# Half-F rows of w4 taken for four token tiles in one excursion, with a fixed order of w3, w4 and attention tiles

## The chip, the cores and the metric

The kernel runs on one core of a Trainium2 chip. The metric is the device time of one execution in microseconds (us), the median of several. Executions of one kernel scatter by about 1 us (0.4%). The differences at stake are 0.1 to 0.9 us, most of them below what timing alone resolves, so the text uses a second measure, read from the trace of one profiled execution of each kernel. It is called the **stretch**: from the start of the first projection matmul with the weights `wkg` (the matmuls of `wq` for the first tiles come before it) to the start of the last matmul of all. It leaves out the head and the 2.8 us tail. Times within a trace are counted from the start of its own execution; where two traces are compared to a fraction of a us, their heads (before 12.83, after 12.58) have to be taken off, and the text says where it does so.

Engines are named as the profile names them: PE (TensorE matmuls), PEld (TensorE weight loads), DVE (VectorE), ACT (ScalarE), POOL (GpSimd), SP (SyncE). The kernel takes PSUM, which receives the results of matmuls, as eight **banks** of 512 float32 columns in each of 128 partitions.

## The reference, cut to what matters

```python
# S = 2048 tokens, D = 640, F = 1728; 32 heads of 20
q, k, v = split(x @ wqkv);  pq, pk = phi(q), phi(k)
kv = sum_s pk v^T;  z = sum_s pk
a  = (pq @ kv / (pq . z)) @ wo                       # linear attention
x1 = x + shift(gelu(layernorm(x) @ w1)) @ w2
b  = x1 + gelu(layernorm(x1) @ w3) @ w4              # F = 13 * 128 + 64
out = g * a + (1 - g) * b
```

F is thirteen times 128 and a half: the last 64 rows of `w4` (and columns of `w3`) are the **half-F** part. There are 16 token tiles of 128, in four chunks of four tiles.

## The kernel before

Everything is written as *items* in streams. At build, a list scheduler takes the streams' items one at a time, guided by a small model of the engines' times, and so fixes the order of the instructions on every engine. At run time nothing is reordered: an item that the model put too early makes its engine wait. This is the model's wait rule and the rule of choice (`cp` is the longest path of item durations behind an item):

```python
for w in waits:          # in the model: when may this instruction start?
    tw = self.ev_time.get(w, 0.0) + (170.0 if w[0] == sem else SEM_LAT)   # same engine 170 ns, else 60
...
if sem.startswith("d:") and nbytes < 0:                # a DMA transpose
    self.eng_free[eng] = t + 1350.0
    end = t + 2800.0
...
key = (max(est, t_pe), 0 if it["dur"] == 0.0 else 1, -cp[n])              # smallest key is emitted next
```

One token tile of w4 is a `w4_tile`: thirteen matmuls of 512 columns and thirteen of 128. The half-F part comes first, in a `w4_half` for two tiles at a time, with 64-row matmuls in pairs (rows 0 to 63 serve one tile, rows 64 to 127 the other):

```python
def w4_half(t):                                   # t = 0, 2, 4, ... 14: eight excursions
    pr = (t % 4) // 2
    for i in range(2):
        b = pair(); bs += [b, b + 1]; w4_banks[t + i] = (b, b + 1)
    bank_hold.update(bs)                          # four banks held
    for i, (n0, n1) in enumerate(((0, 512), (512, D))):
        for par in range(2):
            rows = slice(64 * par, 64 * par + 64)
            jobs.append((ps[:, bs[2 * par + i], 0:n1 - n0], h2h[rows, t // 4, 128 * pr:128 * (pr + 1)], w4[rows, KFF, n0:n1]))
    ... # one matmul per job, start=True, stop=False

def w4_tile(t):                                   # 13 + 13 matmuls of 128 rows, start=False
    ...
    stt(x_tok[:, t, :], psf[:, 512 * b1:512 * b1 + D], stg[:, 3, t:t + 1], abx[:, sa, :], ALU.mult, ALU.add)  # one eviction; tile 15 in two
```

The attention tile and what must be there before it:

```python
qt_tile(t):  DMA transpose  pqnT[:, :, tile t] <- pq_tok[:, t, :]      # queue of SP; after W2 tile 15 and transpose 15 of xn
a_tile(t):   10 matmuls of pqnT[:, j, tile t] with M_sb; eviction into abx on VectorE
```

`pqnT` needs `pq_tok` divided by its denominators (query normalisation: `qs`, then `qn`, on VectorE). And the SP queue serves the transposes in order: the first `pqnT` comes behind the last of 16 transposes of the normalised `x1` (`xnT<-xn`), which hangs on this chain: W2 tile (PE) → its eviction into `x_tok` (VectorE) → squares (ScalarE) → statistics (GpSimd) → normalisation into `xn`, a **ring of 3 buffers** (GpSimd) → transpose (SP's queue).

## Time and profile before

| | before |
|---|---|
| median of 3 runs | 265.46 us (265.42 to 265.71) |
| profiled execution, span | 264.6 us |
| PE busy | 258.2 us, 98% of the span |
| share of PE in the chain that ended last | 96% |
| stretch | 248.967 us |
| PE waits within the stretch | none |

The first three lines are the page's span, its busy table and its table of the chain that ended last.

```profile
span 264.6 us, 4264 instructions
PE 258.2 (98%) x1675; PEld 136.4 (52%) x1707; DVE 145.9 (55%) x242; ACT 107.6 (41%) x216; POOL 91.1 (34%) x148
PE 96%; DMA 1%; issue 1%; ACT 0%; DVE 0%
```

The groups of instructions by line with shapes kept apart: line, engine, operation, out<-in, partitions x elements, count | busy us, mean ns of one | idle us before them and its releaser.

```profile
L1085 PE MATMUL ps<-w_84,h2h 64*128 64x512 bf16 x16 | 3.1, 386 | 0.0
...
L645 DVE SCALAR_TENSOR_TENSOR x_tok<-ps,stg,abx 128x640 bf16<-128x640 f32 x15 | 13.2, 883 | 48.8 <-PE ps L1103 48.8
```

The mean of the matmuls (386 ns) is no cost: matmuls overlap, and their ends are modelled. What a matmul costs is the distance between starts, 216 ns for 512 columns and 56 ns for 128 in this trace. That agrees with the Trainium skill, "TensorE: Matmul & The Clock Gate" (Wait — 56ns, not 53.3ns?), which gives 215.7 and 55.6 ns for back-to-back matmuls on the warm array.

The cost at issue stands in the timeline of PE around an excursion (start us, duration us, engine, line, operation, count):

```profile
173.34 1.24 PE L606 MATMUL ps<-xnT,w_58 128*128 128x512 bf16 x5
174.51 0.45 PE L1085 MATMUL ps<-w_84,h2h 64*128 64x512 bf16 x4
174.89 1.47 PE L1103 MATMUL ps<-w_84,h2T 128*128 128x512 bf16 x6
```

Five matmuls of 216 ns from 173.34 should let the next start at 174.42; the 64-row pair starts at 174.51, about 0.09 us late. A pair of 512 columns and a pair of 128 take 0.216 + 0.056 us (the two matmuls of a pair, on different rows, start 3 ns apart here), so the next full matmul should start at 174.78; it starts at 174.89. Read from single starts in nanoseconds, an entry costs 95 to 97 ns, an exit 92 to 93, and the second pair after an entry and the second matmul after an exit start another 10 to 11 late (227 ns after the one before them instead of 216). These are **mode switches**; the Trainium skill, "TensorEngine Tiling (Array Packing)" (Key Properties), says that changing the tiling mode drains TensorE, and gives no number. Eight such excursions exist.

The waits of PE: engine, line, waited for: us in total, times, longest us.

```profile
PE ps L834 <- POOL ones_c L665: 1.6, 1, 1.6
PE ps L1103 <- issue: 0.3, 2, 0.2
...
PE ps L606 <- issue: 0.2, 1, 0.2
```

The first belongs to the head, as does the line left out. The two with "issue" are lone gaps of exactly one matmul (216 ns) where a matmul's record is missing from the trace (1675 records of 1707), not waits. So after its head PE never waits in this kernel. The first attention tile:

```profile
138.72 1.03 PE L606 MATMUL ps<-xnT,w_58 128*128 128x512 bf16 x4
139.58 2.60 PE L606 MATMUL ps<-M_sb,pqnT 128*128 128x512 bf16 x14
```

It starts directly after the w3 matmuls before it. Its transpose is the first in this line of the timeline of SP (merged, eight of them):

```profile
135.28 10.54 SPq L279 DMA_TRANSPOSE pqnT<-pq_tok  x8
```

It was issued at 135.28 us and took 2.7 us to land, so it was there at about 138.0: a slack of 1.5 us, which no table of waits shows.

### The profile page before, as it was taken

The page shows a single profiled execution, that of the slowest core. Times are in us where ns is not written, and L with a number is a line of the kernel's source. Part 1 is how long each engine was busy: PE and PEld are TensorE (multiplying, and loading weights), DVE is VectorE, ACT ScalarE, POOL GpSimd, SP SyncE. Part 2 cuts the span into 40 slices and gives each one's busy share as a digit, 9 for nine tenths or more (in the row PEclk, how much of TensorE's full clock was granted, in tenths as well). Part 3 has the DMA queues.
Part 4 walks back from the last instruction along what each step waited for, and adds up shares of the span by engine and source line. Part 5 has one row for each costly group of instructions (what it writes and reads, how often), then busy time and mean ns, then how long its engine had stood idle before and what let it go on. Part 6 is the DMA issues. An engine that isn't in the chain of part 4 may idle for free.

```text
span 264.6 us, 4264 instructions
## 1 busy us (share of the span) xinstructions
PE 258.2 (98%) x1675; PEld 136.4 (52%) x1707; DVE 145.9 (55%) x242; ACT 107.6 (41%) x216; POOL 91.1 (34%) x148
## 2 busy tenths in 40 slices
PE   7999999999999999999999999999999999999996
PEld 3655555555555454554444545554545455545553
DVE  0397877899903797999786886312212121122242
ACT  3486767742365758675661031212211222121000
POOL 4003996849774017487821104001110011021020
DMA  6775898551666895253666731120000200002011
GB/s 203 244 103 147 205 146 149 162 115 24 102 121 104 299 373 82 54 99 60 69 124 124 110 68 25 33 93 0 2 0 0 102 0 0 2 0 99 2 50 50
DMA packets 50595, 24.77 MB, mean 94 GB/s; under 512 B 41996, under 2 KB 49165, under 8 KB 50576
## 3 DMA queue, kind: packets, MB, share of 16 engines
q1 hardware_dynamic: 49328, 21.23, 36.3%
q0 software_dynamic: 1152, 3.28, 5.4%
q8 instruction: 13, 0.21, 0.3%
q14 instruction: 6, 0.05, 0.1%
q10 hardware_dynamic: 96, 0.00, 0.0%
HBM read 12.05 MB, written 2.62 MB: 55 GB/s over the span
## 4 chain that ended last, share of the span: by engine, by line
PE 96%; DMA 1%; issue 1%; ACT 0%; DVE 0%
PE ps L606 60%; PE ps L1103 21%; PE ps L786 8%; PE ps L858 2%; DMA x_tok<-in_A_x_dram 1%; PE ps L1085 1%; PE ps L1025 1%; PE ps L617 1%; PE ps L859 1%; PE ps L944 1%; DVE x_tok L645 0%; PE ps L834 0%; ACT h2T L662 0%; ACT M_sb L662 0%
## 5 line engine op out<-in xcount | busy, mean ns | idle before, releaser
L662 ACT ACTIVATE h2T<-ps 128x512 bf16<-128x512 f32 x52 | 31.0, 597 | 86.5 <-PE ps L606 86.5
L606 PE MATMUL ps<-xnT,w_58 128*128 128x512 bf16 x250 | 59.0, 379 | 0.5
L1103 PE MATMUL ps<-w_84,h2T 128*128 128x128 bf16 (+1 forms) x412 | 58.2, 298 | 0.4 <-issue 0.3
L628 POOL TENSOR_SCALAR abx<-x_tok,stg 128x640 f32<-128x640 bf16 x16 | 13.9, 874 | 107.6 <-DVE x_tok L645 71.0
L1103 PEld LDWEIGHTS ps<-w_84,h2T 128*128 128x128 bf16 x416 | 32.4, 98 | 27.8 <-issue 2.1
L645 DVE SCALAR_TENSOR_TENSOR x_tok<-ps,stg,abx 128x640 bf16<-128x640 f32 (+2 forms) x17 | 14.3, 844 | 50.7 <-PE ps L1103 50.7
L606 PEld LDWEIGHTS ps<-xnT,w_58 128*128 128x128 bf16 x260 | 24.3, 98 | 24.9 <-issue 0.4
L645 DVE SCALAR_TENSOR_TENSOR abx<-ps,stg,abx 128x640 f32<-128x640 f32 x16 | 14.1, 882 | 28.5 <-PE ps L606 25.5
L662 ACT ACTIVATE Er<-ps 128x640 bf16<-128x640 f32 x32 | 22.4, 704 | 12.7 <-PE ps L606 8.5
L662 ACT ACTIVATE hsT<-ps 128x512 bf16<-128x512 f32 (+1 forms) x32 | 18.9, 593 | 14.6 <-PE ps L606 14.3
L661 ACT ACTIVATE junk<-x_tok 128x640 bf16<-128x640 bf16 x32 | 23.6, 736 | 2.0 <-DVE x_tok L643 1.7
L606 PE MATMUL ps<-M_sb,pqnT 128*128 128x128 bf16 (+1 forms) x157 | 23.7, 298 | 0.2
L606 PE MATMUL ps<-w_60,hsT 128*128 128x128 bf16 (+1 forms) x158 | 23.6, 298 | 0.1
L786 PE MATMUL ps<-pk_tok,x_tok 128*128 128x128 bf16 (+1 forms) x156 | 23.3, 297 | 0.2
L606 PE MATMUL ps<-xnT,w_59 128*128 128x512 bf16 x96 | 23.2, 379 | 0.3 <-issue 0.2
L606 PE MATMUL ps<-wkg,xT 128*128 128x131 bf16 (+1 forms) x148 | 22.4, 298 | 0.1
L606 PEld LDWEIGHTS ps<-M_sb,pqnT 128*128 128x128 bf16 x160 | 13.3, 98 | 12.4 <-issue 0.4
L606 PEld LDWEIGHTS ps<-w_60,hsT 128*128 128x128 bf16 x160 | 13.3, 98 | 12.2
L628 POOL TENSOR_SCALAR xn<-x_tok,st_54 128x640 bf16<-128x640 bf16 x16 | 17.4, 1090 | 4.7 <-DMA xnT<-xn 4.6
L606 PE MATMUL ps<-wq,xT 128*128 128x128 bf16 (+1 forms) x118 | 18.2, 298 | 0.1
L628 POOL TENSOR_SCALAR xn<-x_tok,st_55 128x640 bf16<-128x640 bf16 x16 | 16.3, 1028 | 3.6 <-DMA xnT<-xn 3.2
L628 DVE TENSOR_SCALAR Er<-Er 128x640 bf16<-128x640 bf16 x32 | 12.0, 375 | 9.4 <-ACT Er L662 9.2
(74 smaller groups left out, 264.2 us busy)
## 6 DMA issues: line engine op xcount, KB each, us to landing
w_58<-in_B_w_dram SPq DMA_DIRECT2D x1, 2160.0 KB, 8.2
w_84<-in_B_w_dram SPq DMA_DIRECT2D x1, 2080.0 KB, 13.6
x_tok<-in_A_x_dram SPq DMA_DIRECT2D x3, 640.0 KB, 5.5
out_dram<-x_tok SPq DMA_DIRECT2D x3, 640.0 KB, 3.3
wq<-in_A_wqkv_dram SPq DMA_DIRECT2D x5, 160.0 KB, 4.4
wkg<-in_A_wqkv_dram SPq DMA_DIRECT2D x5, 160.0 KB, 4.4
wv<-in_A_wqkv_dram POOLq DMA_DIRECT2D x1, 800.0 KB, 6.3
wo_aug<-in_A_wo_dram POOLq DMA_DIRECT2D x5, 150.0 KB, 5.1
```

Source lines behind the costliest of these rows:

```text
L606: ins = e.matmul(out_ap, l, r, start=(i == 0), stop=(i == n - 1))
L617: ins = e.transpose(o, s_, ident[:])
L628: return engf(lambda e: e.tensor_scalar(out_ap, in_ap, s1, s2, op0, op1), rd, [out_ap], cost=cost)
L645: return dve(lambda e: e.scalar_tensor_tensor(out_ap, in0, scalar, in1, op0, op1), rd, [out_ap], cost=cost)
L661: return act(lambda e: e.activation(out_ap, in_ap, func, bias=bias, scale=scale, accum_out=accum), rd, wr, cost=cost)
L662: return act(lambda e: e.activation(out_ap, in_ap, func, bias=bias, scale=scale), rd, wr, cost=cost)
L786: ins = e.matmul(o, l, r, start=(t0 + q_ == 0), stop=(t0 + q_ == NT - 1))
L858: e.matmul(ps[:, b, 0:512], l, w[:, k, 0:512], start=(k == 0), stop=(k == KD - 1))
L859: return e.matmul(ps[:, b + 1, 0:n2], l, w[:, k, 512:512 + n2], start=(k == 0), stop=(k == KD - 1))
L944: ins = e.matmul(o, l, r_, start=st_, stop=sp_, skip_group_check=True)
L1025: ins = e.matmul(o, l, r, start=st, stop=sp)
L1103: ins = e.matmul(o, l, r, start=False, stop=(i == KFF - 1))
```

## The change

The intent is to halve the mode switches of w4: one excursion for four tiles, so four of eight go. Six banks are then held: one per tile for the 512 columns, and two banks shared by the 128-column tails of tiles t and t+2. With six banks taken, w3 cannot be woven between w4 tiles, so the order is fixed by new dependencies: all of w3 of the next chunk, then the excursion, then the four w4 tiles with one attention tile between. Besides, every w4 eviction is split in two, and one number of the scheduler's model changes: a VectorE instruction that waits on VectorE is modelled with 40 ns of latency where it had 170.

```diff
-                tw = ... + (170.0 if w[0] == sem else SEM_LAT)
+                tw = ... + ((40.0 if eng == "dve" else 170.0) if w[0] == sem else SEM_LAT)
 def w4_half(t):
-        pr = (t % 4) // 2
-        ...                       # two pairs of banks, four jobs
+        b0, b2, bt = pair(), pair(), pair()
+        tiles = [((b0, b2)[i // 2] + i % 2, bt + i % 2, 128 * (i // 2)) for i in range(4)]
+        bank_hold.update((b0, b0 + 1, b2, b2 + 1, bt, bt + 1))
+            for pr in range(2):
+                for par, tail in ((0, False), (1, False), (0, True), (1, True)):
+                    ...           # tail: start=(pr == 0), shares bank bt + par
+                    ...           # else: start=True
 def w4_tile(t):
-        stt(x_tok[:, t, :], psf[...], ...)                              # tile 15 alone in two
+        stt(x_tok[:, t, 0:512], ps[:, b1, 0:512], ...)
+        stt(x_tok[:, t, 512:D], ps[:, b2, q0:q0 + 128], ...)
 # dependencies
-                if c >= 2: deps.append((("w4", 4 * (c - 2) + 3), 0.0))  # w3 chunk c
+                if c >= 2: deps.append((("a", 4 * c - 1), 0.0))
+            if c == 1 and j == KFF - 3: deps.append((("a", 3), 0.0))
-        if t % 2 == 0: IT.add("W4", ("w4h", t), 0.49, ...)
+        if t % 4 == 0:
+            deps4.append((("w3", min(c + 1, NCH - 1), KFF - 1), 0.0))
+            if t == 0: deps4.append((("a", 3), 0.0))
+        elif t + 3 < NT: deps4.append((("a", t + 3), 0.0))
+        if t % 4 == 0: IT.add("W4", ("w4h", t), 0.76, ...)
... (cut)
```

More of the change, by code (lines that the diff above doesn't have):

```diff
@@ L238, in simulate @@
             for w in waits:
-                tw = self.ev_time.get(w, 0.0) + (170.0 if w[0] == sem else SEM_LAT)
+                tw = self.ev_time.get(w, 0.0) + ((40.0 if eng == "dve" else 170.0) if w[0] == sem else SEM_LAT)
                 if tw > t:
@@ L1068, in w4_half @@
         tag_chk("h2T", sl, t // 4)
-        pr = (t % 4) // 2
-        bs = []
-        for i in range(2):
-            b = pair()
-            bs += [b, b + 1]
-            w4_banks[t + i] = (b, b + 1)
-        bank_hold.update(bs)
-        jobs = []
-        for i, (n0, n1) in enumerate(((0, 512), (512, D))):
-            for par in range(2):
-                rows = slice(64 * par, 64 * par + 64)
-                jobs.append((ps[:, bs[2 * par + i], 0:n1 - n0], h2h[rows, t // 4, 128 * pr:128 * (pr + 1)], w4[rows, KFF, n0:n1]))
+        b0, b2, bt = pair(), pair(), pair()
+        tiles = [((b0, b2)[i // 2] + i % 2, bt + i % 2, 128 * (i // 2)) for i in range(4)]
+        for i in range(4):
+            w4_banks[t + i] = tiles[i]
+        bank_hold.update((b0, b0 + 1, b2, b2 + 1, bt, bt + 1))
         def fn(e):
             ins = None
-            for o, l, r in jobs:
-                ins = e.matmul(o, l, r, start=True, stop=False)
+            for pr in range(2):
+                for par, tail in ((0, False), (1, False), (0, True), (1, True)):
+                    rows = slice(64 * par, 64 * par + 64)
+                    bm, bs, q0 = tiles[2 * pr + par]
+                    l = h2h[rows, t // 4, 128 * pr:128 * (pr + 1)]
+                    if tail:
+                        ins = e.matmul(ps[:, bs, q0:q0 + 128], l, w4[rows, KFF, 512:D], start=(pr == 0), stop=False,
+                                       skip_group_check=True)
+                    else:
+                        ins = e.matmul(ps[:, bm, :], l, w4[rows, KFF, 0:512], start=True, stop=False)
             return ins
-        pe(fn, [h2h[:, t // 4, 128 * pr:128 * (pr + 1)], w4[:, KFF, :]], [j[0] for j in jobs], cost=490.0)
+        pe(fn, [h2h[:, t // 4, :], w4[:, KFF, :]], [ps[:, b, :] for b in (b0, b0 + 1, b2, b2 + 1, bt, bt + 1)], cost=760.0)
     def w4_tile(t):
@@ L1094, in w4_tile @@
         a = t % 4
-        b1, b2 = w4_banks.pop(t)
+        b1, b2, q0 = w4_banks.pop(t)
         def grp(o, n0, n1):
@@ L1102, in fn @@
                 for i, (l, r) in enumerate(prs):
-                    ins = e.matmul(o, l, r, start=False, stop=(i == KFF - 1))
+                    ins = e.matmul(o, l, r, start=False, stop=(i == KFF - 1), skip_group_check=(n0 > 0))
                 return ins
@@ L1106, in w4_tile @@
         grp(ps[:, b1, 0:512], 0, 512)
-        grp(ps[:, b2, 0:128], 512, D)
+        grp(ps[:, b2, q0:q0 + 128], 512, D)
         bank_hold.discard(b1)
-        bank_hold.discard(b2)
-        if t == NT - 1:
-            stt(x_tok[:, t, 0:512], ps[:, b1, 0:512], stg[:, 3, t:t + 1], abx[:, sa, 0:512], ALU.mult, ALU.add)
-            stt(x_tok[:, t, 512:D], ps[:, b2, 0:128], stg[:, 3, t:t + 1], abx[:, sa, 512:D], ALU.mult, ALU.add)
-        else:
-            stt(x_tok[:, t, :], psf[:, 512 * b1:512 * b1 + D], stg[:, 3, t:t + 1], abx[:, sa, :], ALU.mult, ALU.add)
+        if a >= 2:
+            bank_hold.discard(b2)
+        stt(x_tok[:, t, 0:512], ps[:, b1, 0:512], stg[:, 3, t:t + 1], abx[:, sa, 0:512], ALU.mult, ALU.add)
+        stt(x_tok[:, t, 512:D], ps[:, b2, q0:q0 + 128], stg[:, 3, t:t + 1], abx[:, sa, 512:D], ALU.mult, ALU.add)
     def out_tiles(t0, t1):
@@ L1171, in _build @@
                 if c >= 2:
-                    deps.append((("w4", 4 * (c - 2) + 3), 0.0))
+                    deps.append((("a", 4 * c - 1), 0.0))
+            if c == 1 and j == KFF - 3:
+                deps.append((("a", 3), 0.0))
             IT.add("W3", ("w3", c, j), 1.08, lambda c=c, j=j: w3_group(c, j), deps)
@@ L1193, in _build @@
         deps4 = [(("a", t), 0.0), (("w3h", c - c % 2), GEL), (("w3", c, KFF - 1), GEL)]
-        if t % 2 == 0:
-            IT.add("W4", ("w4h", t), 0.49, lambda t=t: w4_half(t), deps=deps4)
+        if t % 4 == 0:
+            deps4.append((("w3", min(c + 1, NCH - 1), KFF - 1), 0.0))
+            if t == 0:
+                deps4.append((("a", 3), 0.0))
+        elif t + 3 < NT:
+            deps4.append((("a", t + 3), 0.0))
+        if t % 4 == 0:
+            IT.add("W4", ("w4h", t), 0.76, lambda t=t: w4_half(t), deps=deps4)
         IT.add("W4", ("w4", t), 3.5, lambda t=t: w4_tile(t), deps=deps4)
```

## The prediction

> **What bounds it now.** TensorE. The page's busy table gives PE 258.2 of 264.6 us (98%); the chain that ended last is 96% PE. Busy PE alone proves little, so I read start times of single matmuls: from 7.7 us to the last (261.8 us) they follow at 216 ns (512 columns) or 56 ns (128 columns). Lone 216 ns extras every 7 to 9 us are missing records. The real extras are mode switches, into and out of matmuls on part of the rows or columns. Otherwise only the head (about 6 us) and the tail (2.8 us after the last matmul starts) are lost.
>
> **What it removes.** The half-F matmuls of w4 (64 rows) run as eight excursions of four (groups by line: 32). Before each, the first pair starts 95 to 97 ns late; after it the next 128-row matmul is 92 ns late, the one after another 10. That is about 200 ns each, 1.6 us in all, and agrees with the Trainium skill ("TensorEngine Tiling (Array Packing)", Key Properties: changing tiling mode drains the TensorE). Four excursions of eight do the same work: 4 x 0.2 = 0.8 us goes, all on the critical path. Inside a merged excursion the second 512 pair follows a 128 pair; its weight load (94 ns) may not hide under 55 ns: up to 40 ns each back. Net -0.65 to -0.8 us.
>
> Tails of tiles t and t+2 share a bank, only the first flagged start; this is what the skill's "PSUM — Partial Sum Buffer" (The four PSUM rules) asks. I expect correct results.
>
> **What it adds.** 15 VectorE evictions split in two: 0.76 + 0.35 us instead of 0.88 (last tile against the others). VectorE is about 20% busy after 174 us (stretch table): free.
>
> **What it moves.** With six banks held, w3 of the next chunk no longer interleaves with w4; one attention tile (1.36 us of PE) stands between w4 tiles (3.5 us). Its pair is evicted about 1.1 us after PE: no wait. Before the first three excursions stand w3 groups of 1.08 us with 0.60 us gelu: banks come free in time. Before the last excursion a w4 tile may come directly, one of its six banks still in eviction (0.76 us, starting 0.5 us before PE is done): estimate 0.2 to 0.4 us of PE wait. The half-F of w3 for chunks 2 and 3 probably lands just before a w4 excursion: one direct mode change instead of two, -0.1 us. In the query normalisation phase (118 to 166 us, VectorE 70 to 85% busy) four attention tiles must come before w3 of chunk 1 ends; evictions queue behind VectorE pieces of up to 1.6 us: 0 to 1 us of new waits. The changed VectorE latency in the scheduler's model is nearer the trace (dependent VectorE instructions follow within 40 ns) and reorders earlier phases a little; PE is saturated there either way.
>
> **Sum.** -0.75 - 0.1 + 0.3 = about -0.6 us from 265.5: 264.9 us; range 264.3 to 266.3. Faster by over 2% (under 260.2) needs idle PE time that does not exist: 1%. Slower by over 2% needs a bank or VectorE jam: 3%. Within 2%: 96%.
>
> **What would show it.** 64-row w4 matmuls still 32, in four runs of eight; eight switches of 92 to 97 ns instead of sixteen; PE share 97 to 98%; PE waits on VectorE under 0.5 us, only before the last excursion; 32 x_tok evictions instead of 17.
>
> **What would make it wrong.** PE waiting before an excursion for six banks, or for attention evictions at 140 to 160 us; w3 waiting for normalised input; a reordering in the first 120 us that opens gaps.

## The result, and the profile after

The result is correct. The median of six runs is 265.78 us (265.2 to 266.18), against 265.65 us (265.42 to 266.42) for the kernel before in the same rounds. Ratios here and below are the mean time of one kernel's fast runs over that of the other's of the same rounds, so not quite the ratio of the medians quoted: 0.9999, 95% interval 0.9979 to 1.0018, the same. (Where the text says faster or slower it means that the interval lies on one side of 1.)

```profile
span 264.4 us, 4289 instructions
PE 259.3 (98%) x1707; PEld 136.3 (52%) x1707; DVE 148.6 (56%) x257; ACT 107.7 (41%) x216; POOL 93.8 (35%) x148
PE 91%; POOL 3%; DMA 2%; DVE 1%; issue 0%; SPq 0%; ACT 0%; POOLq 0%
```

PE's share is 98% as before, and its busy time is even 1.1 us longer, because all 1707 records are there this time. Busy time does not show what follows. The Trainium skill, "Perfetto Trace Analysis" (Identifying the Most-Contended Engine), says of another use of it, judging how close a kernel is to roofline, that matmul busy time is not a good measure; here it does not tell a kernel with 0.87 us of waits from one without. The chain that ended last does show something new: 91% PE, and GpSimd, a DMA and SP's queue within it.

The excursions are as intended: 32 half-F matmuls, four runs of eight, eight switches.

```profile
L1086 PE MATMUL ps<-w,h2h 64*128 64x512 bf16 x16 | 2.6, 381 | 0.1
...
L645 DVE SCALAR_TENSOR_TENSOR x_tok<-ps,stg,abx 128x512 bf16<-128x512 f32 x16 | 12.0, 750 | 64.8 <-PE ps L1104 64.8
L645 DVE SCALAR_TENSOR_TENSOR x_tok<-ps,stg,abx 128x128 bf16<-128x128 f32 x16 | 5.6, 350 | 0.0
```

The timeline of PE at the first of them:

```profile
155.71 0.81 PE L606 MATMUL ps<-xnT,w 128*128 128x512 bf16 x3
156.45 0.39 PE L1086 MATMUL ps<-w,h2h 64*128 64x512 bf16 x2
156.68 0.22 PE L1083 MATMUL ps<-w,h2h 64*128 64x128 bf16 x2
156.73 0.38 PE L1086 MATMUL ps<-w,h2h 64*128 64x512 bf16 x2
156.95 0.22 PE L1083 MATMUL ps<-w,h2h 64*128 64x128 bf16 x2
157.10 1.47 PE L1104 MATMUL ps<-w,h2T 128*128 128x512 bf16 x6
```

The second 512 pair starts at 156.73, 56 ns after the 128 pair at 156.68 (first matmul to first matmul), which is the usual distance for 128 columns: its weight load (94 ns in the trace) costs nothing.

But PE now waits in two places. The waits of PE, and the timeline of PE at both places (in brackets: idle before, and the releaser):

```profile
PE ps L834 <- POOL ones_c L665: 1.6, 1, 1.6
PE ps L606 <- DMA pqnT<-pq_tok: 0.5, 1, 0.5
```

```profile
140.51 2.33 PE L606 MATMUL ps<-xnT,w 128*128 128x512 bf16 x10
143.36 1.31 PE L606 MATMUL ps<-M_sb,pqnT 128*128 128x512 bf16 x6 [0.52 <-DMA pqnT<-pq_tok]
...
245.49 0.39 PE L1086 MATMUL ps<-w,h2h 64*128 64x512 bf16 x2
```

The bracket counts from a modelled end; by the distance of starts the first attention tile is **0.681 us** late. The last excursion at 245.49 starts 282 ns late, 95 of them the switch: **0.187 us** of wait. There the timeline of VectorE shows the two evictions of the w4 tile before it from 244.68 to 245.76, as one of the six banks is still to be emptied:

```profile
244.68 1.08 DVE L645 SCALAR_TENSOR_TENSOR x_tok<-ps,stg,abx 128x512 bf16<-128x512 f32 x2 [1.92 <-PE ps L1104]
```

(The view has merged two instructions and prints the shape of the first. Taken singly they are the tile's 512-column eviction, 750 ns from 244.68 to 245.43, and its 128-column eviction, 351 ns from 245.40. The excursion starts 57 ns after the end of the first one.)

Stretch: 248.994 us, 0.027 more than before. So the stretch as a whole gained nothing; whether the merging itself did is what e_split will show. Where the first wait comes from can be followed in the chain of waits in order of time:

```profile
129.21 0.83 ACT junk L661 x2
...
134.19 4.67 POOL xn L628 x4
138.86 0.79 POOL abx L628
...
140.59 2.72 DMA pqnT<-pq_tok
...
143.36 13.16 PE ps L606 x75
```

PE waits for the first `pqnT` transpose, issued at 140.59 (before: 135.28; with the heads taken off, 5.6 us later). It stands in SP's queue behind the last transposes of `xn`, these behind the last four normalisations on GpSimd, these behind statistics of squares that ScalarE made at 129.2. One step earlier still is the eviction of the last W2 tile on VectorE. PE finishes that tile at 125.44; VectorE does this instead of its eviction:

```profile
125.49 1.08 DVE L1045 TENSOR_TENSOR pq_tok<-pq_tok,dnr 128x640 bf16<-128x640 bf16 x1
126.49 0.81 DVE L636 TENSOR_TENSOR qprod<-pq_tok,zb 128x640 f32<-128x640 bf16 x1
127.34 0.82 DVE L1035 TENSOR_REDUCE dnr<-qprod 128x32 f32<-128x640 f32 x1
128.07 0.81 DVE L643 SCALAR_TENSOR_TENSOR x_tok<-ps,x_tok 128x640 bf16<-128x640 f32 x1
```

The last line is the eviction, 2.6 us after PE was done: a query normalisation and the sums of the next stand in front of it.

### The profile page after: what moved, and what is told of

Its sections match the earlier page's. It is cut to its first block, busy times and chain, and to the rows that moved or that the text cites. A ratio compares the mean times of both kernels' runs of the same rounds, so it can differ in the third digit from the quotient of the medians.

```text
span 264.4 us, 4289 instructions
## 1 busy us (share of the span) xinstructions
PE 259.3 (98%) x1707; PEld 136.3 (52%) x1707; DVE 148.6 (56%) x257; ACT 107.7 (41%) x216; POOL 93.8 (35%) x148
## 4 chain that ended last, share of the span: by engine, by line
PE 91%; POOL 3%; DMA 2%; DVE 1%; issue 0%; SPq 0%; ACT 0%; POOLq 0%
PE ps L606 56%; PE ps L1104 21%; PE ps L786 8%; PE ps L858 2%; POOL xn L628 2%; DMA x_tok<-in_A_x_dram 1%; POOL st L636 1%; DMA pqnT<-pq_tok 1%; PE ps L1086 1%; DVE x_tok L645 1%; PE ps L617 1%; PE ps L944 1%; PE ps L859 1%; PE ps L1025 0%; SPq L279 0%
## 5 line engine op out<-in xcount | busy, mean ns | idle before, releaser
L606 PE MATMUL ps<-xnT,w 128*128 128x512 bf16 x360 | 82.6, 379 | 0.0
L1104 PE MATMUL ps<-w,h2T 128*128 128x512 bf16 (+1 forms) x416 | 58.8, 299 | 0.0
L606 PEld LDWEIGHTS ps<-xnT,w 128*128 128x128 bf16 x360 | 33.8, 98 | 36.0 <-issue 0.4
L1104 PEld LDWEIGHTS ps<-w,h2T 128*128 128x128 bf16 x416 | 32.4, 98 | 25.6 <-issue 1.1
L628 POOL TENSOR_SCALAR xn<-x_tok,st 128x640 bf16<-128x640 bf16 x32 | 35.6, 1122 | 6.7 <-DMA xnT<-xn 6.3
L606 PE MATMUL ps<-M_sb,pqnT 128*128 128x512 bf16 (+1 forms) x160 | 24.4, 299 | 0.5 <-DMA pqnT<-pq_tok 0.5
L606 PE MATMUL ps<-w,hsT 128*128 128x512 bf16 (+1 forms) x160 | 24.3, 299 | 0.0
L786 PE MATMUL ps<-pk_tok,x_tok 128*128 128x512 bf16 (+1 forms) x160 | 23.9, 299 | 0.0
L606 PE MATMUL ps<-wkg,xT 128*128 128x512 bf16 (+1 forms) x150 | 22.6, 299 | 0.0
L606 PE MATMUL ps<-wq,xT 128*128 128x512 bf16 (+1 forms) x120 | 18.3, 299 | 0.0
```

The lines of the kernel that those rows point to most:

```text
L606: ins = e.matmul(out_ap, l, r, start=(i == 0), stop=(i == n - 1))
L628: return engf(lambda e: e.tensor_scalar(out_ap, in_ap, s1, s2, op0, op1), rd, [out_ap], cost=cost)
L786: ins = e.matmul(o, l, r, start=(t0 + q_ == 0), stop=(t0 + q_ == NT - 1))
L1104: ins = e.matmul(o, l, r, start=False, stop=(i == KFF - 1), skip_group_check=(n0 > 0))
```

## The experiments

The theory after this reading was: *merging gives about 0.85 us; the 40 ns of the model, not the fixed order, creates the 0.68 us wait; placing the last excursion directly after a w4 tile costs the 0.19.* Rivals: the merged excursion is worth less than it seems (contention, reloads); the wait comes from the new dependencies or the split evictions; PE would have waited anyway. Twelve kernels were run; all gave correct results. One table for all; each is then told by itself. Every ratio is against the kernel before in the same rounds.

| run | what | stretch us | PE waits in the stretch, ns | median us | ratio, 95% |
|---|---|---|---|---|---|
| (before) | | 248.967 | none | 265.65 | 1 |
| (after) | | 248.994 | 681 + 187 | 265.78 | 0.9999 (0.9979 to 1.0018) |
| e_lat | before, 40 ns | 251.368 | 2391 | 269.82 | 1.0139 (1.0118 to 1.0161) |
| e_170 | after, 170 ns | 248.308 | 187 | 265.08 | 0.9962 (0.9944 to 0.9979) |
| e_split | after, excursions cut in two | 249.839 | about 686 + 190 | 266.27 | 1.0014 (0.9998 to 1.003) |
| e_both | after, two dependencies more | 248.370 | 250 (a new one) | 264.99 | 0.9961 (0.9939 to 0.9982) |
| e_lat_hold | e_lat, first attention tile later | 248.969 | none | 265.58 | 0.9988 (0.997 to 1.0006) |
| e_lat_ring | e_lat, ring of 4 | 248.967 | none | 265.98 | 0.9999 (0.9983 to 1.0015) |
| e_best | e_170, last excursion after last attention tile | 248.119 | none | 264.9 | 0.9951 (0.9937 to 0.9966) |
| e_evict | before, evictions split | 248.969 | none | 266.05 | 0.9998 (0.9983 to 1.0012) |
| after_ring | after, ring of 4 | 248.937 | 619 + 187 | 265.36 | 0.9988 (0.997 to 1.0007) |
| best_m | e_best, two switches fewer in M | 247.911 | none | 264.74 | 0.996 (0.994 to 0.9979) |
| after_qn | after, query normalisation after W2 evictions | 249.540 | 1236 + 187 | 266.08 | 1.0009 (0.9989 to 1.003) |
| after_qn_ring | both of these | 248.304 | 187 | 265.34 | 0.9983 (0.9963 to 1.0004) |

Where two timed kernels lie within 0.5 us the verdict rests on the stretch and on the trace, which are one execution each; the timed ratios agree in sign or contain 1.

### e_lat: the model's 40 ns alone, on the kernel before

```diff
-  (170.0 if w[0] == sem else SEM_LAT)
+  ((40.0 if eng == "dve" else 170.0) if w[0] == sem else SEM_LAT)
```

> The kernel before, with only the VectorE latency of the scheduler's model changed (170 to 40 ns); no merging, no fixed order. Measure: time from the first k-tile matmul to the start of the last matmul in the trace, 248.97 us before and 248.99 us after. My theory (switches saved, 0.87 us of new waits caused by the fixed order): same as before, 248.9 to 249.1, sixteen w4 switches, no PE wait at the first attention tile; time ratio to before 0.999 to 1.001. Rival A (the model's latency alone reorders the early phases and costs what the merging saves): 249.5 to 249.9, with a PE wait of about 0.7 us at the first attention tile.

Measured: stretch 251.368 us, 2.401 more, of it 2.391 in one wait: again the first attention tile, for its transpose (the table of PE's waits has 2.2 us for it). The chain of waits in order of time:

```profile
123.14 4.38 DMA xnT<-xn
127.52 0.09 issue
127.61 0.90 POOL xn L628
128.51 0.73 POOL st L628
...
139.31 2.72 DMA pqnT<-pq_tok
142.08 1.96 PE ps L606 x12
```

One number of a model that no instruction carries makes the kernel 1.4% slower. The tile was placed where it would start at about 139.7, but its transpose was issued only at 139.31. The lateness here has another root than in the kernel after: GpSimd wants to normalise into a ring buffer that a transpose, issued at 123.14, holds until 127.52, 4.38 us instead of the usual 2.7 (the page's table of DMA issues has a median of 2.7). GpSimd stands 2.77 us, and the last chunk's statistics queue behind. The timed loss (about 3.7 us by the medians, against 266.14 of before in that batch) is larger than the 2.4 us of the trace. The traced execution alone took 268.84 us, 2.7 more than that median, and its granted clock was 1.000; in the other four (269.49 to 270.54 us) it was 0.994. The missing 0.6% of 267 us would be 1.6 us (an estimate), so the larger loss goes with these four. Of them there is no trace, so whether the PE gap causes the lower clock stays open.

What follows: the 40 ns alone is enough to create a wait of this kind. It does not yet show that it creates that of the kernel after, whose order is another.

### e_170: the kernel after with 170 ns restored

```diff
-  ((40.0 if eng == "dve" else 170.0) if w[0] == sem else SEM_LAT)
+  (170.0 if w[0] == sem else SEM_LAT)
```

> The changed kernel with the model's latency put back to 170 ns. In its order the first attention tile stands about 1.2 us later on PE. My theory: the 0.68 us wait of PE on the pqnT transposes at the first attention tile shrinks to under 0.2 us, because that tile is issued later, while W2 still runs late as in the changed kernel; the 0.19 us wait for banks before the last excursion stays: stretch 248.3 to 248.6. Rival B (the wait belongs to the fixed order whatever the latency says): wait 0.5 us or more, 248.9 to 249.1.

Measured: stretch 248.308, the wait at the first attention tile gone, the 187 ns before the last excursion still there. Timed 0.9962 (0.9944 to 0.9979). Here VectorE takes the last W2 tile first:

```profile
125.91 0.82 DVE L643 SCALAR_TENSOR_TENSOR x_tok<-ps,x_tok 128x640 bf16<-128x640 f32 x1
...
126.66 0.18 DVE L628 TENSOR_SCALAR dnr<-dnr 128x32 f32<-128x32 f32 x1
```

The eviction starts at 125.91, where PE was done with the tile at 125.65; the normalisation comes after. The first `pqnT` transpose is issued at 138.71 instead of 140.59, and the attention tile stands about 1.1 us later in PE's order. Two things move at once, so this run shows that the 40 ns is necessary for the wait, and not yet by which of the two. With the heads taken off, the first transpose lands 2.1 us earlier than in the kernel after, and PE comes to the tile 1.1 us later.

### e_split: the merged excursions cut in two again

The six banks, their holding, the shared tails and the order stay; the second half of the excursion becomes an item of its own before the third tile. In the last chunk that half is also made to wait until the last attention tile is issued.

```diff
-            for pr in range(2):
+            for pr in (pr_,):
+        if t % 4 == 2:
+            IT.add("W4", ("w4g", t), 0.49, lambda t=t: w4_half_row(t - 2, 1), deps=deps4)
```

> The changed kernel, same order, same six banks, but each merged excursion cut in two: tiles 0 and 1 before the first w4 tile, tiles 2 and 3 before the third; the last attention tile moves before the second half of the last chunk. My theory: eight more switches, 4 x 0.2 = 0.8 us more than the changed kernel: stretch 249.7 to 249.9, ratio to the kernel before about 1.003. Rival C (the drain of a mode switch costs nothing in the end, merging was worthless and the balance is chance): 248.9 to 249.1.

Measured: 249.839, which is 0.845 more than the kernel after, with waits together 8 ns longer: 4 x 0.21 us. (At the first attention tile the gap is 902 ns, of it 216 a missing record.) The timeline of PE shows the cut excursion; a switch stands on both sides of each:

```profile
155.71 0.39 PE L1094 MATMUL ps<-w,h2h 64*128 64x512 bf16 x2
155.94 0.22 PE L1091 MATMUL ps<-w,h2h 64*128 64x128 bf16 x2
156.09 1.47 PE L1115 MATMUL ps<-w,h2T 128*128 128x512 bf16 x6
```

So merging is worth 0.845 us, four times 211 ns: 95 to 96 for the entry, 10 to 11 on the second pair after it, 92 to 93 for the exit, 10 to 11 on the second matmul after it, and the 3 by which the later matmul of a pair follows the first. This kernel has the gain undone and both waits kept, and it is slower than before in the trace (+0.872): the two waits do not come from the merging itself.

### e_both: both waits attacked by dependencies

```diff
+        if t == 0:
+            deps.append((("w3", 1, 6), None))      # first attention tile later
+            if t == 12:
+                deps4.append((("a", 15), 0.0))     # last excursion after the last attention tile
```

> The changed kernel with both new waits taken away by order alone: the first attention tile goes after two more w3 groups of chunk 1, and the last excursion goes after the last attention tile. My theory: PE waits at 143 and 245 us gone, 0.87 us less: stretch 248.0 to 248.3, ratio to before about 0.997 (264.8 us where before has 265.6). Rival D (a wait taken away here comes back later, since VectorE and the banks are the true limit in that phase): 248.7 to 249.1.

Measured: both old waits gone, 248.370; but a new one of 250 ns before the first excursion at 156.31. Its VectorE timeline:

```profile
155.17 0.88 DVE L645 SCALAR_TENSOR_TENSOR abx<-ps,stg,abx 128x640 f32<-128x640 f32 x1 [1.00 <-POOL abx L628]
155.97 0.17 DVE L628 TENSOR_SCALAR dnr<-dnr 128x32 f32<-128x32 f32 x1
```

The excursion wants six of eight banks, and the attention tile's pair is only being emptied from 155.17 to 156.05. This is the "bank" wait that the prediction feared, and it appears only when the attention tile is pushed late. The table of waits names `dnr` as releaser; it was `abx`, one instruction earlier: its semaphore came at 156.06 and PE's sequencer went on at 156.09, before `dnr` ended at 156.14. A dependency added in this scheduler also changes `cp` of everything before it, so the order elsewhere moved too; later experiments at the first attention tile hold items back without touching priorities.

### e_lat_hold: e_lat with the first attention tile held back

```diff
-                if pos[s_] >= len(lst):
+                if pos[s_] >= len(lst) or (lst[pos[s_]] == ("a", 0) and ("w3", 1, 5) not in done):
```

> e_lat (before plus the 40 ns latency) lost 2.39 us in one PE wait: the first attention tile is issued 2.4 us before its pqnT transpose has landed (issued at 139.31, landed at 142.0). Here that tile is held back in the order until three more w3 groups (3.2 us of PE) have been issued; everything issued before it is the same. My theory (the loss is only the place of that tile in PE's fixed order, no engine lacks capacity): wait under 0.1 us, stretch from the first k-tile matmul to the last matmul start 248.9 to 249.2 as before, ratio to before 0.998 to 1.002. Rival E (the phase is truly limited by VectorE and GpSimd, so the wait comes back as another one): stretch 250 or more.

Measured: 248.969, no wait, the stretch of the kernel before to 2 ns. Placing alone repairs e_lat: its transposes are as late as in e_lat (first one issued at 138.55; with the heads taken off, 0.1 us later than in e_lat), and PE does not mind.

### e_lat_ring: e_lat with four buffers for the normalised tiles

```diff
-    xn = pa.alloc("xn", [128, 3, D], BF16)
+    xn = pa.alloc("xn", [128, 4, D], BF16)
-        sx = slot("xn", 3)
+        sx = slot("xn", 4)
```

> e_lat with four buffers for the normalised tile instead of three; the order of all engines is the same, only a wait goes. In e_lat GpSimd sat 2.77 us before the twelfth normalisation until the transpose three tiles earlier had landed, and the statistics of the last chunk queue behind it. If that is a link of the chain that makes the first attention tile late: its transpose is issued about 1.6 us earlier (137.7 instead of 139.3) and the PE wait falls from 2.39 to 0.5 to 1.1 us, stretch 249.5 to 250.1. Rival F (the link is VectorE, whose order puts query normalisation before the last W2 evictions, or ScalarE; the buffer does not matter): wait stays above 2 us, stretch 251 or more.

Measured: the order on every engine is that of e_lat, and the wait is gone altogether: 248.967. The first `pqnT` transpose is issued at 135.88 instead of 139.31 (with the heads taken off, 2.6 us earlier). The direction was expected, the size was missed: I had left 0.5 to 1.1 us of wait. So in e_lat the shortage of ring buffers is what turns a late landing into a wait of PE; the later W2 evictions alone (the last starts at 123.81 in e_lat, 122.24 before) are not enough: in e_lat_ring they use up 1.3 of the 1.5 us of slack. It is one traced execution; the median of six, 265.98, against 269.82 for e_lat says the same.

### e_best: e_170 with the last excursion after the last attention tile

```diff
# to e_170
+            if t == 12:
+                deps4.append((("a", 15), 0.0))
```

> The changed kernel with the old 170 ns latency (e_170) and the last excursion placed after the last attention tile; against e_170 only that block moves. My theory: the 0.19 us wait for the sixth bank goes, nothing else changes: stretch 248.1 (e_170 had 248.31), no PE wait over 0.1 us after 10 us, ratio to before about 0.9955. Rival G (the last attention tile there makes the excursion wait for its eviction, or the last evictions come later): stretch 248.3 or more.

Measured: 248.119 (248.1 was expected), no waits. Around the last excursion:

```profile
244.09 1.52 PE L606 MATMUL ps<-M_sb,pqnT 128*128 128x512 bf16 x10
245.55 0.39 PE L1086 MATMUL ps<-w,h2h 64*128 64x512 bf16 x2
```

The attention tile fills the time in which the bank is emptied. Timed 0.9951 (0.9937 to 0.9966), so faster than before by about 0.5%; the stretch is 0.848 us (0.34%) shorter, which is the 0.845 of the merging.

### e_evict: the split of the evictions alone, on the kernel before

```diff
-        if t == NT - 1:
+        if True:
```

> The kernel before with every w4 eviction split in two as in the change (512 and 128 columns), eight excursions, nothing else edited; two w3 groups change places around 142 to 160 us. My theory: VectorE has room, so stretch 248.9 to 249.1 as before and no PE wait. Rival H (the split costs VectorE time where it is busy, 140 to 165 us, and PE waits for a bank): stretch 249.3 or more.

Measured: 248.969, ratio 0.9998. Fifteen more VectorE instructions, nothing on PE's path. The split is free here, and in the order of before it is no cause; the waits at the first attention tile and before the last excursion also go with the split left in (after_qn_ring, e_best).

### after_ring: the kernel after with four buffers

Edit as in e_lat_ring.

> The changed kernel itself with four buffers for the normalised tile instead of three; all engines have the same order as in the changed kernel. My theory: its 0.68 us PE wait at the first attention tile hangs on the same chain as in e_lat (normalisation waits for a buffer, statistics and transposes queue behind it, pqnT last), so the wait goes and only the 0.19 us wait before the last excursion stays: stretch 248.3, ratio to before 0.996 to 0.998. Rival (in the changed kernel W2 itself ends too late, at 125 us instead of 120, and the buffers are not the link): wait stays over 0.4 us, stretch 248.7 or more.

Measured: the same order on every engine, first `pqnT` transpose still late, 619 ns of 681 stay (248.937). My theory that the ring explained the wait here as it did in e_lat fell. In the kernel after, the last statistics are late because of VectorE, and a fourth buffer helps only what comes before them.

### after_qn: the kernel after with the query normalisation behind the last W2 eviction

```diff
-                if pos[s_] >= len(lst):
+                if pos[s_] >= len(lst) or (lst[pos[s_]] == ("qn", 7) and ("w2", 15) not in done) \
+                   or (lst[pos[s_]] == ("w3", 1, 6) and ("a", 0) not in done):
```

The second condition keeps PE's order what it is in the kernel after; without it the scheduler would move the attention tile.

> The run with four buffers left the changed kernel's wait at 0.62 us, so there the link is another one. In its trace the last W2 eviction on VectorE starts at 128.07, 2.6 us after W2 is done on PE (125.44), behind one whole query normalisation (five instructions, 124.82 to 128.16); in e_170 it starts at 125.91. Here the order puts that normalisation after the last W2 eviction; PE's order is the same as in the changed kernel. Theory: the last statistics, transposes and the first pqnT transpose come 1.5 to 2 us earlier (139.0 instead of 140.6), the 0.68 us wait goes, stretch 248.3 (changed kernel 248.99), ratio to before 0.996 to 0.998. Rival (the chain has yet another link behind it, GpSimd or the transposes): the wait stays over 0.3 us, stretch 248.6 or more.

Measured: the wait did not go, it grew: the gap before the first attention tile is 1.452 us above the usual distance of starts, of which 0.216 is a missing record (it is missing at the same place in after_qn_ring, which does not wait there), so 1.236 us of wait. The stretch says the same: 249.540 against 248.304 for after_qn_ring, a difference of 1.236. The timeline of GpSimd says why:

```profile
124.36 2.60 POOL L628 TENSOR_SCALAR xn<-x_tok,st 128x640 bf16<-128x640 bf16 x3
129.41 0.88 POOL L628 TENSOR_SCALAR xn<-x_tok,st 128x640 bf16<-128x640 bf16 x1 [2.45 <-DMA xnT<-xn]
```

GpSimd sat 2.45 us before the twelfth normalisation, for a ring buffer whose transpose landed 4.06 us after its issue; the last chunk's statistics queued behind it. That is the cause seen in e_lat. As a statement that VectorE's order alone makes the wait, my theory fell.

### after_qn_ring: both

> Both links at once. With the VectorE order alone the last eviction came 2.3 us earlier, yet the wait grew to 1.45 us, because GpSimd then sat 2.45 us before the twelfth normalisation until a transpose had landed (4.06 us after its issue), with the last statistics queued behind it; with four buffers alone the wait stayed at 0.62 us, because VectorE's eviction was late. Here both are taken away, with PE's order as in the changed kernel. Theory (two links in series, each hidden behind the other): the first pqnT transpose is issued at 138 to 139.5 us instead of 140.6, the wait at the first attention tile goes (under 0.1 us), stretch 248.3, ratio to before 0.996 to 0.998. Rival (a third link): wait over 0.3 us.

Edit: the two above together. Measured: the wait at the first attention tile is gone, 248.304 (248.3 was expected), the 187 ns remain. The first `pqnT` transpose is issued at 138.44 (after: 140.59), with PE's order unchanged; the line is from the timeline of SP (merged, six transposes). Timed 0.9983 (0.9963 to 1.0004).

```profile
138.44 7.87 SPq L279 DMA_TRANSPOSE pqnT<-pq_tok  x6
```

So, in the one traced execution of each, the wait of the kernel after has two links, each of which keeps it when the other is cut: the order on VectorE and the ring of three with transposes that land late. With both cut it is gone. All of it in one table, with the heads taken off (us from the start of the stretch); the slack is the time from landing to need, less 0.05 us that PE takes to start after a landing, and where it is negative it is the wait:

| run | last W2 matmul starts on PE | last W2 eviction starts | first `pqnT` landed | PE could start the tile | slack |
|---|---|---|---|---|---|
| before | 107.2 | 109.4 | 125.2 | 126.8 | 1.5 |
| e_lat | 107.2 | 110.9 | 129.1 | 126.8 | -2.4 |
| e_lat_ring | 107.2 | 110.9 | 126.5 | 126.8 | 0.2 |
| e_170 | 112.6 | 113.1 | 128.6 | 131.2 | 2.5 |
| after | 112.6 | 115.5 | 130.7 | 130.1 | -0.7 |
| after_ring | 112.6 | 115.4 | 130.7 | 130.1 | -0.6 |
| after_qn | 112.6 | 112.9 | 131.3 | 130.1 | -1.2 |
| after_qn_ring | 112.6 | 112.9 | 128.6 | 130.1 | 1.4 |

### best_m: e_best with the last M group in another order

In the last group of the product of `kv` with `wo` two pairs have 120 rows and 40 rows. Before: 512 columns of 120 and 40 rows, then 128 columns of 120 and 40 (four switches). Here: 512 and 128 columns of 120 rows, then both of 40 rows (two switches).

```diff
+        if j == KD - 1:
+                for i, (pi, r) in enumerate(prs):
+                    for o, n0, n1 in ((ps[:, b1, 0:512], 0, 512), (ps[:, b2, 0:128], 512, D)):
+                        ins = e.matmul(o, Lt[0:nrow(r), pi, :], wo_aug[0:nrow(r), r, n0:n1], ...)
```

> e_best with the four partial matmuls of the last M group ordered by rows (both of 120 rows, then both of 40) instead of 120, 40, 120, 40. A test of the theory on a switch the change never touched: two switches fewer, at 0.10 us each, 0.2 us: stretch 247.9 (e_best 248.12), no new wait, ratio to before about 0.995. If a change of row count alone is not what costs the 0.1 us, the stretch stays at 248.1.

Measured: 247.911, 0.208 less than e_best (247.9 was expected): two switches of 95 and 92 ns in place of four of 96, 103, 107 and 102. No waits. Timed 0.996 (0.994 to 0.9979), the shortest stretch of all. Like e_170, e_both and e_best it is timed below the kernel before with its whole interval, and its stretch is shorter than those of before and after. Among these four the timing does not decide; the trace favours best_m.

## Why the prediction was right or wrong

The time was predicted at 264.9 us with 264.3 to 266.3 as range; it came out at 265.78, inside the range and "within 2%", to which 96% was given. But the forecast gain of 0.6 us did not come: it would be a ratio of 0.9977, just outside the measured interval (0.9979 to 1.0018), and the measured sum in the trace is about nothing. That the range held is partly luck: it reached up to 266.3 for waits of up to 1 us behind VectorE, which did not come, and a wait of another kind, 0.68 us, filled that room. Against the ledger, in us of stretch:

| term | predicted | measured | shown by |
|---|---|---|---|
| four excursions fewer | -0.8, less up to 40 ns for each reload: -0.65 to -0.8 | -0.845 | e_split against after |
| half-F of w3 next to an excursion | -0.1 | -0.1 and +0.1 | traces of before and after |
| wait before the last excursion | +0.2 to 0.4 | +0.187 | trace; gone in e_best |
| waits at attention tiles 140 to 160 us, behind VectorE | 0 to 1 | 0 there | trace |
| wait for the first attention tile's transpose | not in the sum | +0.681 | trace; gone in e_170 and after_qn_ring |
| sum | -0.6 | +0.02 by these terms, +0.027 measured | after against before |

Point by point:

- **PE bounds the kernel, and switches are its only reducible cost**: right. 8 x 95 ns and 8 x 92 ns stand in the trace, and merging is worth 4 x 0.211 us. But in the kernel after PE also waits (see the step that failed).
- **Reloads inside a merged excursion, up to 40 ns each**: wrong in size, the cost is zero (56 ns from the 128 pair to the second 512 pair, as without a load between).
- **Correctness of shared tails**: right, results are correct in all runs of it. It is what the Trainium skill, "PSUM — Partial Sum Buffer" (The four PSUM rules), lets one expect of a bank whose first matmul alone carries the start flag.
- **Split evictions free**: right (e_evict).
- **Half-F of w3, -0.1**: right where it was looked at (one direct change of mode of 96 ns at 192 us). Its mirror was overlooked: before, the half-F of w3 for chunks 0 and 1 at 135.13 us stood directly after the 40-row matmul of M, and shared its switch; in the new order it doesn't, one switch more, +0.1.
- **0.2 to 0.4 us before the last excursion**: right at its lower edge, 0.187 (e_best removes it, and only it, from e_170).
- **"PE waits on VectorE under 0.5 us, only before the last excursion"**: true as written; the larger new wait is on a DMA, and so was not looked for.

**The step that failed** is this sentence: "The changed VectorE latency in the scheduler's model is nearer the trace (dependent VectorE instructions follow within 40 ns) and reorders earlier phases a little; PE is saturated there either way." The first half is true: in 48 places of each of the two traces where a VectorE instruction follows one whose result it needs (the reciprocal, the product after it, the sums), it starts 34 to 35 ns after that one's end. The second took PE's saturation before the change for a property of the phase. It is a property of the order: the first attention tile had 1.5 us of slack behind a transpose, set by where the model placed it. The larger part of the delay is the fixed order's, which puts 35 w3 matmuls before the end of W2 where there were 10: with the heads taken off, W2 is done on PE 5.4 us later, with 170 ns and with 40 alike. By itself that does no harm, because PE then comes to the first attention tile 4.4 us later too, and e_170 has 2.5 us of slack. The 40 ns takes 3.2 us of it: the query normalisation passes the last W2 eviction on VectorE and the first transpose lands 2.1 us later, while PE comes to the tile 1.1 us earlier. Against the kernel before, the transpose lands 5.5 us later and PE comes only 3.3 us later. The slack of 1.5 us is gone, and 0.68 us of wait stand in its place. I looked for the risk at the other end of the tile, in the eviction (VectorE queue), while it lay at its input.

What is shown, each in one traced execution: under the fixed order the 40 ns is necessary for the wait (e_170), and in the order of before it is sufficient for one of its kind (e_lat); the fixed order without it makes none at that tile (e_170); placement alone removes e_lat's (e_lat_hold); the ring alone removes e_lat's (e_lat_ring), but not that of the kernel after (after_ring), nor does the order of VectorE (after_qn); both do (after_qn_ring). Argued from the schedule and not shown by a run: that the 40 ns reorders VectorE *because* the model believes the normalisation ends sooner. Open: why one and the same transpose lands in 2.7 us in most cases and in 4.1 to 4.4 us around 123 to 128 us in e_lat and after_qn. The late landings are not peculiar to these runs: the kernel before has one of 4.64 us, issued at 122.82. The packet times in the 14 kept traces give a strong hint. Of the 672 transposes of `xn` and `pq_tok`, 115 took over 3.5 us, and every one of these had a transfer of 8 or 16 KB on the queues that the profile calls `instruction` (the program's own instructions being fetched) in flight within 2.7 us of its issue; of the 457 without such a transfer none took over 3.5 us. (100 transposes had one and landed sooner, 56 of them in under 3 us.) No run moved a fetch, so that it is the cause is not shown. Open too is why four of five executions of e_lat had the lower clock that goes with its larger timed loss.

## What to carry to other kernels

A schedule that is fixed at build by a model is part of the kernel: make a change to the model a run of its own, since one that brings the model nearer the trace cost 1.4% here (e_lat). Before claiming that an engine at 98% cannot be hurt by reordering, list for each of its inputs that comes through a queue (here: the transposes) the landing time and the start of its user, and keep the smallest slack in view; the table of waits shows only slack that is already gone. And when two experiments that each cut one link fail, cut both before dropping the theory: here the one half-cure even made it worse.

## What the Trainium skill lacked or had wrong

- "TensorEngine Tiling (Array Packing)", Key Properties, gives no cost of a mode switch: here 95 to 97 ns going in and 92 to 93 going out for 64 rows, 93 in and 96 out for 64 columns, 92 to 107 where 40 rows or columns are on one side, and 10 to 11 ns more on the second matmul (or pair) after the change. Going from 128 to 120 rows and back cost nothing (0 to -1 ns). The page lists modes of 128, 64 and 32 rows; it does not say to which of them 120 or 40 rows belong.
- "TensorE: Matmul & The Clock Gate" contradicts itself: Back-to-back issue gap gives about 81 ns (128 columns) and 131 ns (512 columns) as the sustained spacing of matmuls that each have a weight load, and calls 56 and 216 ns the gap of isolated ones, where its section Wait — 56ns, not 53.3ns? has these as measured back to back. Here streams with a weight load for each matmul ran at 56 and 216 ns throughout the stretch (1707 loads, 1707 matmuls).
- No page has a measured spacing for 64-row pairs with a weight load between them: here the second 512 pair followed the 128 pair after 56 ns, as without a load, so the load is hidden.
- "DMA: Bandwidth & Descriptors" has a bandwidth for DMA transposes but no time from issue to landing for one small one: here 2.7 us for a 128x640 tile of 2-byte elements (median), over 3.5 and up to 4.7 us in 115 of 672 cases, and one about every 1.3 us on one queue. No page connects such late landings with instruction fetches, which were in flight in all 115.
- "TensorE: Matmul & The Clock Gate" (What's actually happening) has the clock fall after at least one idle window of about 3.4 us. In e_lat, with a PE gap of 2.4 us in the trace, four of five executions had a mean granted clock of 0.994, the traced one 1.000, and all eleven executions of the kernel before in that batch 1.000. Whether the gap was longer in those four, or a shorter one is enough, no run here shows.
